# Pooled attention and routed attention experts on one core: queries four tokens to a partition, turned on VectorE, scores in four row tiles

## The chip, the core and the metric

The kernel runs on one core of a Trainium2 chip, in one launch. The metric is the device time in microseconds; a figure for a kernel is the median of its runs. TensorE is called PE, VectorE DVE, ScalarE ACT, GpSimd POOL and SyncE SP, as in the profile.

## What is computed

Two blocks in a row, for B = 8 batches, H = 8 heads, S = 576 tokens and D = 64. The first is attention over keys and values pooled by eight, so 72 keys. Its output, 512 wide, is the input x of the second: four causal attention experts with a head width of 64, of which each token takes the two with the highest gate.

```python
def _attn_ref(q, k, v):
    k_p = k.reshape(B, H, 72, 8, D).mean(axis=3)
    v_p = v.reshape(B, H, 72, 8, D).mean(axis=3)
    attn = softmax(q @ k_p.transpose(0, 1, 3, 2) / 8)
    return attn @ v_p

def _moe_ref(x, w_gate, wq, wk, wv, wo):      # x: (8, 576, 512)
    logits = x @ w_gate                       # 4 experts
    topk = the two highest; w = softmax of their logits
    for e in range(4):
        a = softmax(causal((x @ wq[e]) @ (x @ wk[e]).T / 8))
        out += w[e] (0 where e is not chosen) * (a @ (x @ wv[e]) @ wo[e])
```

## The kernel before

The order of the work is written out by hand: a string SEQ (L561 on) of some 1100 tokens, `name:batch@bank`. Each token calls a small function that issues instructions, and each engine runs its own instructions in the order of the string. A `d` at the end puts a copy on DVE rather than ACT, a `c` cuts a matmul into four column tiles of 32. The whole PSUM is one tile of eight banks, and the number after `@` is the bank that a token's matmuls write. The batches are staggered: while the experts of one batch run, the attention of the next ones is under way.

Per batch, in the order of the data:

- `L` (L109): loads from HBM with a cast to bf16, issued on POOL. Keys and values come in 3 chunks each, two tokens to a partition (96 partitions, 768 pieces of 128 elements a chunk); queries in 6 chunks of 96 tokens, 768 pieces of 64 elements each. Three buffers of each kind (NRAW).
- `PK`/`kc` (L222): pooling as a matmul with a fixed matrix, three column tiles side by side; the 72 pooled keys lie in 96 rows. Then the copy to SBUF. `KT`/`kt` (L237): four flips (matmuls with the identity) turn the pooled keys, two heads at a time, into kpT with 128 rows of head dimensions. `PV`/`vc` do the same pooling for values.
- `Q`/`r` (L246): for each of the four head pairs, six flips of 96 tokens into a PSUM bank, and a copy of 576 columns into qT (24 of the 32 copies on DVE, 8 on ACT).
- `E`/`es` (L255): scores, transposed (keys on partitions). Per head pair two matmuls with 64 rows each, side by side in two row tiles, into two banks; one exp of 1024 elements reads both banks into eta. The 64 tail tokens (512 to 575) of all heads go last: eight matmuls of 64 columns, two exps.
- `D`, `dn`, `dx`, `O`, `ov` (L283 to L319): denominators by a matmul with a constant, their inverse by ln and exp on ACT, the product with the values, and the scaled result into xT.
- `P`/`p` (L390): projections to q and k of the experts; `V`/`vg` (L321): values and gate logits.
- `gate` (`g0` to `g9`, L336): exp of the logits on ACT (`g0`), then on DVE the second highest of four by max and min, a mask, weights and their normalisation: nine more steps.
- `S`/`sb` (L412): the experts' scores, 64-row tiles, exps on ACT; `am` (`a`, L440): causal masks by affine_select on POOL.
- `B` (L466), `bv` (L477): weights times values; on DVE the reciprocal (`bz`), its product with the gate (`bg`, L484) and the scaled copy (`b`, L489).
- `T`/`t`: flips and copies; `Y`/`y`: the output projection, a copy to `ofin`, and the store, on SP's queue.

`H` tokens are warm-up matmuls on zeros that write a bank nobody reads (51 of them, all in the first 25 us). `W` loads the experts' weights on POOL, `c` reorders them. A PE "form" below means the shape in which the array is used: 128 rows by 128 or 32 columns, or 64 rows by 128 columns in two row tiles (E and S). Which form a token has follows from its function: H, KT, Q, T, Y, and P, V without `c`: 128 by 128; PK, PV, D, O, and tokens with `c`: 32-column tiles; E and S: 64-row tiles.

The softmax here doesn't subtract the row's maximum and nothing guards it: scores larger than these inputs give would overflow.

## Time and profile before

| what | value |
|---|---|
| runs, us | 166.84, 167.1, 168.86; median 167.1 |
| span of the profiled execution | 165.0 us |
| last output matmul starts, last store is issued | 160.4 us, 161.2 us |
| granted PE clock, mean | 0.996 |
| busy: PE, ACT, DVE, POOL | 157.0, 135.0, 123.8, 104.9 us |
| DVE: copies of query flips | 24 of 0.45 us |
| ACT: copies of query flips | 8 of 0.65 us |
| ACT: main exps of the pooled scores | 32 of 1.02 us; tails 16 of 0.38 us |
| POOL: load issues | 48 of q at 0.775 us, 48 of k and v at 0.78 us |
| POOL: causal masks | 72 of 0.41 us |
| DMA queue of the loads | 78928 packets, 15.21 MB |

The page gives busy times by engine, forty slices of the span, and groups of instructions by line. A group line has the count, the busy time, the mean of one in ns, and the idle time ahead of it with what ended it. Matmuls overlap: each lasts some 0.2 to 0.4 us from start to end, while the next starts much earlier, so prices on PE are read from start to start in the timeline. The table by stretches gives, for each stretch, its length, then the busy us of PE, PEld (weight loads), DVE, ACT and POOL with the number of instructions, then the granted PE clock, the DMA share and GB/s. About one matmul record in twenty is missing from this trace; counts are therefore taken from the code.

### The profile page before, as it was taken

How to read it: one execution, taken by the hardware profiler on the slowest of the kernel's cores; microseconds unless marked ns; L12 is line 12 of the kernel's file. 1: busy time of each engine (PE TensorE's matmuls, PEld its weight loads, DVE VectorE, ACT ScalarE, POOL GpSimd, SP SyncE). 2: the span in 40 equal slices, each digit the busy share in tenths (PEclk: the TensorE clock that was granted, in tenths of full speed). 3: DMA queues.
4: the chain of work that ended last, by engine and by line, in shares of the span. 5: the costliest groups of instructions: out<-in, count | busy, mean ns of one | idle time of the engine just before them, and what ended most of it. 6: DMA issues, size and time to landing. Idle time of an engine off the chain costs nothing. (4 is left out here: it accounts for less than half of the span.)

```text
span 165.0 us, 6106 instructions
## 1 busy us (share of the span) xinstructions
PE 157.0 (95%) x2463; PEld 93.8 (57%) x2463; DVE 123.8 (75%) x410; ACT 135.0 (82%) x247; POOL 104.9 (64%) x178
## 2 busy tenths in 40 slices
PE   6999988999999999999999999999999999999980
PEld 2344354568557656654754878555647686555730
DVE  1101497589799859976988899998998989779960
ACT  3029758999998999888998997789997999898860
POOL 6999891899999999965959997400140211364100
PEclk9999999999999999999999999999999999999998
DMA  2999999999999999999999999923113043055875
GB/s 22 160 153 171 164 172 178 170 145 139 177 156 173 164 157 148 156 233 217 206 178 226 168 198 83 174 100 86 47 68 127 4 131 127 0 190 195 257 260 191
DMA packets 84204, 25.04 MB, mean 152 GB/s; under 512 B 79312, under 2 KB 79568, under 8 KB 84176
## 3 DMA queue, kind: packets, MB, share of 16 engines
q0 software_dynamic: 78928, 15.21, 110.6%
q1 hardware_dynamic: 5024, 9.05, 15.9%
q8 instruction: 19, 0.31, 0.7%
q10 hardware_dynamic: 224, 0.39, 0.6%
q14 instruction: 9, 0.07, 0.1%
HBM read 30.42 MB, written 9.44 MB: 242 GB/s over the span
## 5 line engine op out<-in xcount | busy, mean ns | idle before, releaser
L433 ACT ACTIVATE etb_97<-psum 128x1024 bf16<-128x1024 f32 x24 | 23.6, 1023 | 2.5 <-PE psum L185 2.4
L433 ACT ACTIVATE etb_98<-psum 128x1024 bf16<-128x1024 f32 x24 | 23.5, 1027 | 1.3 <-PE psum L185 1.1
L450 POOL TENSOR_SCALAR_AFFINE_SELECT etb_98<-etb_98 128x256 bf16<-128x256 bf16 x32 | 12.5, 410 | 17.4 <-ACT etb_98 L433 17.2
L450 POOL TENSOR_SCALAR_AFFINE_SELECT etb_97<-etb_97 128x256 bf16<-128x256 bf16 x32 | 12.4, 415 | 15.8 <-ACT etb_97 L433 15.7
L173 PE MATMUL psum<-warm 128*128 128x512 bf16 x51 | 15.2, 443 | 1.8 <-DVE onesd L146 1.3
L273 ACT ACTIVATE eta_91<-psum 96x1024 bf16<-96x1024 f32 x16 | 15.9, 1018 | 1.1 <-PE psum L185 1.1
L273 ACT ACTIVATE eta_92<-psum 96x1024 bf16<-96x1024 f32 x16 | 15.6, 1020 | 0.7 <-PE psum L185 0.6
L117 POOL DMA_DIRECT2D qraw_68<-in_q_dram x18 | 13.9, 775 | 1.2 <-PE psum L185 1.1
L176 DVE COPY ofin<-psum 128x512 f32<-128x512 f32 (+1 forms) x18 | 11.9, 673 | 3.2 <-PE psum L185 2.4
L117 POOL DMA_DIRECT2D qraw_69<-in_q_dram x18 | 13.8, 770 | 0.5 <-issue 0.5
L176 DVE CAST qk_99<-psum 128x512 bf16<-128x512 f32 (+1 forms) x16 | 10.5, 670 | 3.8 <-PE psum L185 3.6
L176 DVE CAST qk_100<-psum 128x512 bf16<-128x512 f32 (+1 forms) x16 | 10.5, 654 | 3.5 <-PE psum L185 3.5
L176 ACT COPY ofin<-psum 128x512 f32<-128x512 f32 (+1 forms) x19 | 10.7, 580 | 2.7 <-PE psum L185 1.8
L185 PE MATMUL psum<-wvg,xT_96 128*32 128x260 bf16 (+1 forms) x120 | 10.8, 275 | 0.0
L173 PEld LDWEIGHTS <-warm 128*128 128x128 bf16 x51 | 5.1, 111 | 9.5 <-issue 5.8
L185 PE MATMUL psum<-wvg,xT_95 128*32 128x260 bf16 (+1 forms) x156 | 10.5, 275 | 0.0
L185 PEld LDWEIGHTS <-etb_97 128*128 128x128 bf16 x240 | 8.8, 97 | 2.0 <-issue 0.4
L117 POOL DMA_DIRECT2D qraw_70<-in_q_dram x12 | 9.2, 784 | 0.0
L185 PEld LDWEIGHTS <-etb_98 128*128 128x128 bf16 x240 | 8.3, 97 | 1.4 <-issue 0.8
L185 PE MATMUL psum<-qk_100 64*128 64x64 bf16 (+4 forms) x96 | 8.8, 276 | 0.1
L117 POOL DMA_DIRECT2D kraw_71<-in_k_dram x9 | 7.0, 787 | 2.7 <-DMA qraw_70<-in_q_dram 1.8
L185 PE MATMUL psum<-qk_99 64*128 64x64 bf16 (+4 forms) x96 | 8.4, 277 | 0.0
(198 smaller groups left out, 452.8 us busy)
## 6 DMA issues: line engine op xcount, KB each, us to landing
out_dram<-ofin SPq DMA_DIRECT2D x31, 256.0 KB, 3.0
kraw_71<-in_k_dram POOLq DMA_DIRECT2D x9, 192.0 KB, 6.2
qraw_68<-in_q_dram POOLq DMA_DIRECT2D x18, 96.0 KB, 5.3
vraw_74<-in_v_dram POOLq DMA_DIRECT2D x9, 192.0 KB, 5.5
kraw_72<-in_k_dram POOLq DMA_DIRECT2D x9, 192.0 KB, 5.9
qraw_69<-in_q_dram POOLq DMA_DIRECT2D x18, 96.0 KB, 5.5
vraw_75<-in_v_dram POOLq DMA_DIRECT2D x9, 192.0 KB, 4.9
kraw_73<-in_k_dram POOLq DMA_DIRECT2D x6, 192.0 KB, 6.5
```

The lines of the kernel that those rows point to most:

```text
L117: nc.gpsimd.dma_start(out=dst, in_=src)
L173: nc.tensor.matmul(out=psum[:, bank, :], lhsT=warm[:, 0:128], rhs=warm[:], start=True, stop=True)
L176: (nc.vector.tensor_copy if dve else nc.scalar.copy)(out=out, in_=in_)
L185: nc.tensor.matmul(out=out, lhsT=lhsT, rhs=rhs, start=start, stop=stop)
L273: nc.scalar.activation(out=eta[:, hp, :, 0:MAIN], in_=psum[0:KR, bank : bank + 2, :], func=EXP, scale=ATT_EXP_SCALE,)
L433: nc.scalar.activation(out=et[:, ep, :, eo : eo + n], in_=psum[:, bank : bank + 2, 0:n], func=EXP, scale=MOE_EXP_SCALE,)
L450: nc.gpsimd.affine_select(out=blk, in_=blk, pattern=[[0, 2], [1, 128]], compare_op=ISGE, fill=0.0, base=0, channel_multiplier=-1,)
```

## The change

1. Queries are loaded four tokens to a partition (128 partitions, pieces of 256 elements), four heads a load: two loads a batch instead of six. The 64 tail tokens of four batches share one buffer, 32 partitions a batch, one load each.
2. `Q` and `r` are gone. A DVE transpose of 32x32 blocks of 4-byte words (`U`, three for a batch's halves and the shared tails: 18 in all) turns the queries: a word is a pair of neighbouring head dimensions, so each 32-partition group then holds 32 pairs, and the even and odd dimensions lie interleaved in the free dimension.
3. Scores run in four row tiles of 32 rows. Each row tile has the tokens of its own partition group; even and odd dimensions are two accumulating matmuls of 128 columns. A half batch (four heads) is 32 matmuls into four banks, a batch's tails are 16 matmuls of 64 columns in one row tile. Each row tile needs the keys of every head and parity in its own 32 rows, so kpT holds four copies, rotated by 32 rows.
4. For batches 0, 1 and 2 the rotated copies are made by flips (16 instead of 4) from a key buffer that holds the first columns twice (`kd`); for batches 3 to 7 by six small SBUF-to-SBUF DMAs on SP (`R`). PK's columns are sorted into even and odd dimensions.
5. The exps read PSUM in the token order (`j r h p t`), so their reads step 32 elements; main exps keep 1024 elements, tails become one exp of 512.
6. The gate's steps after the exp (except `g7`, `g8`) and `bg` move from DVE to POOL; the mask comes from the differences of all pairs of logits.
7. The staging buffers of the weights lie in the output buffers oT.
8. SEQ is written anew: other places, banks and engines for nearly all tokens. Warm-ups 51 to 40; load tokens 96 to 72. Copies on ACT and DVE, before and after: y 18 and 17, then 21 and 14 (the last one is split on both); p 8 and 32, then 12 and 28; t 3 and 21, then 8 and 16; v 14 and 22, then 10 and 26; kc 5 and 3, then 7 and 1; kt 5 and 3, then 3 and 8; and three kd on DVE.

```diff
-    qraws = bufs(NRAW, [KR, NQC, H, D], BF16, "qraw")
+    qraws = bufs(NRAW, [128, H, QT, D], BF16, "qraw")
+    qtls = bufs(B // QUAD, [128, H, 2, D], BF16, "qtl")
+    qTts = bufs(B // QUAD, [128, H, 2, 32, 2], BF16, "qTt")
     kraws = bufs(NRAW, [KR, 3, H, 2, D], BF16, "kraw")
     vraws = bufs(NRAW, [KR, 3, H, 2, D], BF16, "vraw")
-    kps = bufs(2, [KR, H * D], BF16, "kp")
-    kpTs = bufs(2, [128, NHP, KR], BF16, "kpT")
+    kps = bufs(2, [KR, NHP, 224], BF16, "kp")
+    kpTs = bufs(2, [128, NRG, NHP, KR], BF16, "kpT")
     vps = bufs(2, [KR, H, D], BF16, "vp")
-    qTs = bufs(8, [128, S], BF16, "qT")
-    etas = bufs(2, [KR, NHP, 2, S], BF16, "eta")
+    qTs = bufs(2, [128, H, QT, 32, 2], BF16, "qT")
+    etas = bufs(2, [KR, H, S], BF16, "eta")
...
         if nm == "q":
-            dst = qraws[b % NRAW][:, c, :, :]
-            src = q[b, :, KR * c : KR * (c + 1), :].rearrange("h p d -> p h d")
+            hs = slice(NHP * c, NHP * c + NHP)
+            dst = qraws[b % NRAW][:, hs].rearrange("p h t d -> p h (t d)")
+            src = q[b, hs, 0:MAIN, :].rearrange("h (p t) d -> p h (t d)", t=QT)
+        elif nm == "t":
+            dst = qtls[b // QUAD][32 * c : 32 * c + 32].rearrange("p h t d -> p h (t d)")
+            src = q[b + c, :, MAIN:S, :].rearrange("h (p t) d -> p h (t d)", t=2)
...
-    def pool_pe(b, bank, raw, mat):
+    def pool_pe(b, bank, raw, mat, split):
         for t in range(2):
             for c in range(3):
-                mm(psum[32 * c : 32 * c + 32, bank, :], mat[:, :], raw[:, c, :, t, :],
-                   start=(t == 0), stop=(t == 1))
+                x = raw[:, c, :, t, :]
+                if split:
+                    x = x.rearrange("p h (x u) -> p h u x", u=2)
+                mm(psum[32 * c : 32 * c + 32, bank, :], mat[:, :], x, start=(t == 0), stop=(t == 1))
...
-        copy(dve, kps[b % 2][:], psum[0:KR, bank, :])
+        copy(dve, kps[b % 2][:, :, 0:128], psum[0:KR, bank, :].rearrange("j (a n) -> j a n", a=NHP))
+
+    def kd(b, bank, dve):
+        copy(dve, kps[b % 2][:, :, 128:224], psum[0:KR, bank, :].rearrange("j (a n) -> j a n", a=NHP)[:, :, 0:96])
...
     def KT(b, bank):
-        for hp in range(NHP):
-            flip(half_bank(bank)[:, KR * hp : KR * hp + KR],
-                 kps[b % 2][:, 128 * hp : 128 * hp + 128])
-
-    def kt(b, bank, dve):
-        copy(dve, kpTs[b % 2][:],
-             half_bank(bank)[:, 0 : NHP * KR].rearrange("p (a n) -> p a n", a=NHP))
-
-    def Q(b, bank, hp):
-        for c in range(NQC):
-            flip(half_bank(bank)[:, KR * c : KR * (c + 1)],
-                 qraws[b % NRAW][:, c, 2 * hp : 2 * hp + 2, :].rearrange("p h d -> p (h d)"))
-
-    def r(b, bank, dve, hp):
-        copy(dve, qTs[4 * (b % 2) + hp][:], half_bank(bank)[:, 0:S])
-
-
-    def Es(b, bank, hp):
-        for i in range(NHP) if hp == NHP else [hp]:
-            c0, n, at_ = (MAIN, TAIL, TAIL * i) if hp == NHP else (0, MAIN, 0)
-            for hh in range(2):
-                r0 = hh * D
-                mm(psum[0:KR, bank + hh, at_ : at_ + n], kpTs[b % 2][r0 : r0 + D, i, :],
-                   qTs[4 * (b % 2) + i][r0 : r0 + D, c0 : c0 + n])
-
-    def es(b, bank, dve, hp):
-        eta = etas[b % 2]
-        if hp == NHP:
-            for hh in range(2):
-                nc.scalar.activation(
-                    out=eta[:, :, hh, MAIN:S],
-                    in_=psum[0:KR, bank + hh, 0 : NHP * TAIL].rearrange("p (a n) -> p a n", a=NHP),
-                    func=EXP, scale=ATT_EXP_SCALE,
-                )
-        else:
+        for i in range(NRG if b in TURNED else 1):
+            for hp in range(NHP):
+                c = 32 * (-i % NRG)
+                o = KR * (NHP * (i % 2) + hp)
+                flip(half_bank(bank + i // 2)[:, o : o + KR], kps[b % 2][:, hp, c : c + 128])
+
+    def kt(b, bank, dve, part=0):
+        n = 2 if b in TURNED else 1
+        copy(dve, kpTs[b % 2][:, 2 * part : 2 * part + n],
+             half_bank(bank + part)[:, 0 : n * NHP * KR].rearrange("p (k a n) -> p k a n", k=n, a=NHP))
+
+    def spread(b):
+        for k in range(1, NRG):
+            n = 32 * (NRG - k)
+            for d0, s0, m in ((32 * k, 0, n), (0, n, 128 - n)):
+                nc.sync.dma_start(out=kpTs[b % 2][d0 : d0 + m, k], in_=kpTs[b % 2][s0 : s0 + m, 0])
+
+    def turn(b, i):
+        if i == 2:
+            dst, src = qTts[b // QUAD][:], qtls[b // QUAD][:]
+        else:
+            hs = slice(NHP * i, NHP * i + NHP)
+            dst, src = qTs[b % 2][:, hs], qraws[b % NRAW][:, hs]
+        nc.vector.transpose(out=dst.rearrange("p h s x t -> p (h s x t)").bitcast(U32),
+                            in_=src.rearrange("p h s d -> p (h s d)").bitcast(U32))
+
+    def Es(b, bank, u):
+        def score(r, h, t, out, qT):
+            rows = slice(32 * r, 32 * r + 32)
+            nc.tensor.matmul(
+                out=out, lhsT=kpTs[b % 2][rows, (r - 2 * (h % 2) - t) % NRG, h // 2, :],
+                rhs=qT[rows, h, :, :, t].rearrange("p s x -> p (s x)"),
+                start=(t == 0), stop=(t == 1), tile_position=(32 * r, 0),
+            )
+
+        for h in range(H) if u == NHP else range(NHP * u, NHP * u + NHP):
+            for t in range(2):
+                if u == NHP:
+                    score(b % QUAD, h, t, psum[0:KR, bank, TAIL * h : TAIL * h + TAIL], qTts[b // QUAD])
+                else:
+                    o = 128 * (h % NHP)
+                    for r in range(NRG):
+                        score(r, h, t, psum[0:KR, bank + r, o : o + 128], qTs[b % 2])
+
+    def es(b, bank, dve, u, half=None):
+        if u == NHP:
             nc.scalar.activation(
-                out=eta[:, hp, :, 0:MAIN], in_=psum[0:KR, bank : bank + 2, :],
+                out=etas[b % 2][:, :, MAIN:S].rearrange("j h (p t) -> j h p t", t=2),
+                in_=psum[0:KR, bank, :].rearrange("j (h t p) -> j h p t", h=H, t=2),
+                func=EXP, scale=ATT_EXP_SCALE,
+            )
+            return
+        for r in range(2 * half, 2 * half + 2) if SPLIT else [2 * half]:
+            n = 1 if SPLIT else 2
+            nc.scalar.activation(
+                out=etas[b % 2][:, NHP * u : NHP * u + NHP, 128 * r : 128 * (r + n)].rearrange(
+                    "j h (r p t) -> j r h p t", r=n, t=QT),
+                in_=psum[0:KR, bank + r : bank + r + n, :].rearrange("j r (h t p) -> j r h p t", h=NHP, t=QT),
                 func=EXP, scale=ATT_EXP_SCALE,
             )
 
...
         elif step == 1:
-            L2 = L.rearrange("p c (a b) -> p c a b", b=2)
-            for nm, op in (("hi", MAXOP), ("lo", MINOP)):
-                nc.vector.tensor_tensor(
-                    out=tmp(nm, 2, 1), in0=L2[:, :, :, 0:1], in1=L2[:, :, :, 1:2], op=op
-                )
+            nc.gpsimd.tensor_sub(
+                out=tmp("Df", E, E), in0=L.unsqueeze(3).to_broadcast([128, n, E, E]),
+                in1=L.unsqueeze(2).to_broadcast([128, n, E, E]),
+            )
         elif step == 2:
-            for nm, src, op in (("s2", "hi", MINOP), ("s3", "lo", MAXOP)):
-                nc.vector.tensor_tensor(
-                    out=tmp(nm, 1), in0=got(src)[:, :, 0, :], in1=got(src)[:, :, 1, :], op=op
-                )
+            nc.gpsimd.tensor_scalar(out=got("Df"), in0=got("Df"), scalar1=0.0, scalar2=None, op0=ISLT)
         elif step == 3:
-            nc.vector.tensor_tensor(
-                out=tmp("m2", 1), in0=got("s2"), in1=got("s3"), op=MAXOP
+            nc.gpsimd.tensor_add(
+                out=got("Df")[:, :, :, 0:2], in0=got("Df")[:, :, :, 0:2], in1=got("Df")[:, :, :, 2:4]
             )
         elif step == 4:
-            nc.vector.tensor_tensor(
-                out=tmp("msk", E), in0=L, in1=got("m2").to_broadcast([128, n, E]), op=ISGE
+            nc.gpsimd.tensor_add(
+                out=got("Df")[:, :, :, 0], in0=got("Df")[:, :, :, 0], in1=got("Df")[:, :, :, 1]
             )
         elif step == 5:
-            nc.vector.tensor_mul(out=tmp("W", E), in0=got("Ex"), in1=got("msk"))
+            nc.gpsimd.tensor_scalar(
+                out=tmp("msk", E), in0=got("Df")[:, :, :, 0], scalar1=2.0, scalar2=None, op0=ISLT
+            )
+            nc.gpsimd.tensor_mul(out=tmp("W", E), in0=got("Ex"), in1=got("msk"))
...
         if step == "bz":
             nc.vector.reciprocal(out=rz, in_=o[:, :, :, HD : HD + 1])
         elif step == "bg":
-            nc.vector.tensor_mul(
+            nc.gpsimd.tensor_mul(
                 out=gt[:, :, :, 0], in0=rz[:, :, :, 0],
                 in1=at[b // 2, "G"][:, p0:p1, 2 * ep : 2 * ep + 2].rearrange("p c e -> p e c"),
...
+        I:0 J:0 L_k1:0 K:0 L_k0:0 L_k2:0 H14:0@7 PK:0@7 kc:0 kd:0d H4:0@6 KT:0@6 L_q1:0 M:0 L_q0:0
+        kt1:0d L_t1:0 L_v2:0 U0:0 L_t3:0 kt0:0 H7:0@5 E0:0@4 U1:0 E1:0@0 L_v0:0 e01:0 L_v1:0 e00:0
+        e10:0 L_t0:0 L_t2:0 PV:0@4 vc:0d D0:0@5 e11:0 H3:0@7 O01:0@4 O11:0@0 L_k2:1 d0:0 U2:0 L_k1:1
+        D1:0@1 x0:0 o01:0 d1:0 O00:0@5 x1:0 L_k0:1 E4:0@2 O10:0@3 o10:0 H2:0@7 PK:1@4 kd:1d L_q1:1
+        e4:0 D2:0@7 W1:0 U1:1 O20:0@2 o00:0 kc:1 H3:0@6 KT:1@3 kt0:1 kt1:1d L_q0:1 d2:0 x2:0 W0:0
...
```

## The prediction

> **What bounds the kernel now.** I read the page's busy shares and slices first, then the table by stretches, then PE's timeline, because everything hangs on what PE does between its matmuls. The chain that ended last is of no use here: it covers only the last 1.2 us.

> ```profile
> span 165.0 us, 6106 instructions
> ...
> PE 157.0 (95%) x2463; PEld 93.8 (57%) x2463; DVE 123.8 (75%) x410; ACT 135.0 (82%) x247; POOL 104.9 (64%) x178
> ...
> PE   6999988999999999999999999999999999999980
> ```
> PE is busy from about 30 us to the end. But matmuls overlap, so "busy" hides waits. The table by stretches (busy us of PE, PEld, DVE, ACT, POOL) shows who is near its own limit:

> ```profile
> 24.00:32.00 8.00, 7.34 (x126) 3.90 (x123) 5.75 (x16) 6.85 (x13) 4.24 (x8) 1.00 1.81 176
> ...
> 50.00:60.00 10.00, 9.95 (x139) 6.46 (x140) 8.24 (x29) 8.97 (x17) 9.89 (x17) 1.00 2.00 164
> ...
> 100.00:110.00 10.00, 9.92 (x153) 6.46 (x153) 9.50 (x29) 7.72 (x15) 4.60 (x9) 1.00 1.01 108
> ```
> From 50 to 60 us POOL (loads and masks) is as full as PE; ACT runs at 0.9. PE's timeline gives the real prices, start to start:

> ```profile
> 28.22 0.38 PE L185 MATMUL psum<-xT_95,wkp_122 128*128 128x512 bf16 x1
> 28.53 0.23 PE L185 MATMUL psum<-qk_99 64*128 64x64 bf16 x4
> 28.60 0.21 PE L185 MATMUL psum<-qT_87,kpT_80 64*96 64x64 bf16 x2
> 28.65 0.21 PE L185 MATMUL psum<-qT_88,kpT_80 64*96 64x64 bf16 x2
> 28.69 0.21 PE L185 MATMUL psum<-qT_89,kpT_80 64*96 64x64 bf16 x2
> 28.74 0.21 PE L185 MATMUL psum<-qT_90,kpT_80 64*96 64x64 bf16 x2
> 28.78 0.40 PE L185 MATMUL psum<-qT_89,kpT_80 64*96 64x512 bf16 x2
> 29.11 0.40 PE L185 MATMUL psum<-xT_95,wkp_123 128*32 128x512 bf16 x4
> ```
> and later, from all engines' timeline:

> ```profile
> 73.42 0.44 PE L194 MATMUL psum<-ident,osc_108 128*128 128x128 bf16 x5
> ...
> 73.70 0.61 PE L185 MATMUL psum<-wvg,xT_96 128*128 128x260 bf16 x4
> ```
> A 512-column matmul, or a set of tiles side by side, takes 0.2155 us; a pair of 64-column score tails with 96-column weights 45 ns; a 128-column flip 55 ns (five in 0.28 us). From 28.22 to 28.53 is 0.31 us for one 0.2155 us matmul: going from 128-row to 64-row form costs 94 ns, and the way back at 29.11 about the same. The records hold 97 such changes of form.

> **PE's sum now.** Walking the order string with these prices (96-column flip 42 ns, 65-column matmul 29 ns, 260 columns 111 ns): P 31.2 us, V 16.0, Y 15.5, B 14.1, warm-ups 51 x 0.2155 = 11.0, S 10.8, E 8.3, Q 192 x 0.042 = 8.1, O 7.5, PK and PV 6.9, T 4.4, D 3.8, KT 1.3: 139.0 us, and 97 changes x 0.1 = 9.7: 148.7 us. Set against the recorded starts, PE's lateness (start minus work so far) is 1.3 us at the start, 6.8 at the first projection (26.23 us), 7.2 at 40 us and 11.8 at the last output matmul (160.03 us). So PE bounds, behind a ramp fed by the loads.

> [...] here only two row tiles are seen, starting 3 ns apart. [...] no row of this trace reads PSUM with a stride at length.

> **The change on PE.** Query flips go: -8.1 us. Main scores: per batch 4 pairs x 0.2155 = 0.86 us become 16 sets of four 128-column tiles x 55 ns = 0.88: +0.1 over all. I take 55 because the 45 ns of weights seen in the tails fit under it; if weights and matmul add (45 + 53), it is +5.5 us. Tails: 4 pairs x 45 ns become 16 matmuls in one row tile, one after another, x 45 ns: 0.72 - 0.18 = 0.54 a batch, +4.3. Turned keys: 12 more flips in three batches, 36 x 42 ns = +1.5. Warm-ups 51 to 40: -2.4. The new order has 115 changes of form instead of 97 (scores no longer share a form with the experts' scores): +1.8. Sum -2.7: 146.0 us. PK's sorted columns I leave at 0.2155. A half batch of scores now holds four of the eight banks, two of them for two exps (2.0 us), where a pair held two for one; the flips' bank goes instead. I put nothing for it, since the order gives PE other matmuls meanwhile; without them each of the 16 would cost up to 1 us.

> **The loads.** These set the ramp.

> ```profile
> 1.36 2.42 POOL L117 DMA_DIRECT2D kraw_71<-in_k_dram  x3 [0.85 <-POOLq L689]
> ...
> 4.05 4.59 POOL L117 DMA_DIRECT2D qraw_68<-in_q_dram  x6
> 8.64 2.29 POOL L117 DMA_DIRECT2D vraw_74<-in_v_dram  x3
> ```
> The packets between 2 and 40 us come at 0.175 MB/us where they are 256 bytes (k, v, weights) and 0.154 where 128 (q); a batch of k, q or v is 0.59 MB. That puts k at 8.0, q at 11.9 (PE's last wait for it ends at 12.20), v at 15.2 (PV at 15.9), the q weights at 23.9 (copied at 24.46): the stream, not its issue, is the limit. New q packets are 512 bytes; not seen, between 0.175 and 0.21; I take 0.187. Then q lands at 10.8, but the tails of four batches (0.26 MB) come before v ends (14.9), k of batch 1 at 19.1, its second half of q at 20.5, the k weights at 22.0. Behind that lie PK 0.4, copy 0.6, flips 0.7, copy 0.8: first projection at about 23.3 us, 2.9 earlier. But later loads bind too (the same rates, going on down the list of L and W tokens), because the new order puts all keys of batch 3 before half of batch 2's queries: keys of 2 at 33.1 against 25.4 us of PE work ahead of them, keys of 3 at 37.9 against 30.0, queries of 2 at 39.3 plus a turn against 32.0, values of 2 at 45.1 against 37.1. Lateness is then 8.3 at about 40 us, not 7.2: +1.1.

> **The other engines.** DVE: 24 query copies x 0.45 = -10.8; gate steps -12.7 and bg -6.4 (36 x 0.18) go to POOL; 18 turns are added. [...] the 128x512 f32 copy takes 0.687 us: 18 x 0.69 = +12.4 (at twice that, +24.8: still below now). With moved copies (y, p, t, v: -4.4; kc, kd, kt, c: +3.5) about 105 of 123.8. ACT: 8 query copies x 0.65 = -5.2, tail exps 16 x 0.38 to 8 x 0.59 = -1.4, moved copies +4.3: about 133 of 135. POOL: 48 query loads x 0.775 become 24 of about 0.73 (a 256-descriptor load took 0.712): -19.7; each batch gains eight gate instructions and 36 bg in all. [...] Even. These cost nothing while B's results wait behind the 0.9-full ACT and other PE work[...]. What queues behind a waiting bg on POOL is masks and loads; behind the masks waits B. DVE's 15% relief should take as much off the late drift: 0 net. SP: 5 x 6 small copies of keys; first scores follow the key copy by 6.6 us of PE work or more, against 3.0 us of landing for outputs: hidden; beyond 6.6 us each adds to E. Weight staging in oT is free: oT is first written by flips of batch 0's output, long after the weights are copied out.

> **Sum.** -2.7 + 1.1 = -1.6 us: the profiled execution goes from 165.0 to 163.4. The median of the runs is 2.1 us above its span, so 167.1 becomes 165.5.

> **Rivals.**
> - *Likeliest, 165.5 (own range 163 to 168), chance 0.50*: as summed.
> - *The ramp and the waits shrink, 162.5, 0.26*: 512-byte packets at 0.21 take 0.3 us off each half batch and lateness stays at 7.2; the drift of 4.6 us to the end falls to 3 with DVE at 105 and fewer loads ahead of masks: -2.7 - 0.2 - 1.6 = -4.5. For: POOL 9.89 of 10 at 50 us. Against: ACT is as full as before.
> - *Strided exps, slower, 0.14*: the 32 main exps read PSUM four bytes in every 128. ACT's rows (0.59 us for 512, 1.02 for 1024 elements) give 0.84 ns an element; a halved rate adds 0.86 x 32 + 3 = 30 us, ACT 163 us from 12 us on: about 180. ACT has some 16 us of idle time, scattered; from about 1.3 us an exp it decides. Against: no engine row here shows such a loss.
> - *Row tiles do not run together, 0.08*: 64 x 55 ns a batch instead of 16 is +21 us: 186; break-even is 21 ns more per set of four.
> - Rest 0.02.

> **Numbers.** About 2% (3.3 us) is what a measurement of this kernel tells from no change. Below 163.8: 0.16 of the first case and nearly all of the second: 0.33. Above 170.4: the last cases, 0.21. Between: 0.46. The range 160 to 172 leaves out the two slow mechanisms at full size and little of the second case.

> **What would show it.** Right: sets of four score tiles 55 ns apart; tails 45; 115 changes at 94 ns; first projection near 23.3 us; lateness near 8.3 at 40 us and 12 to 13 at the end; exps at 1.02 us; turns at 0.69. Wrong: exps above 1.1, sets above 75 ns, POOL gaps ended by PSUM work with loads late behind them, or E waiting for SP's copies.

## The result, and the profile after

The changed kernel takes 177.7 us (median of four runs, 176.93 to 179.18) against 167.0 before: 1.062 times, 95% interval 1.056 to 1.068. It is slower. The prediction was 165.5, with a range from 160 to 172. Medians and ranges are over all runs of a kernel; ratios leave out runs over 1.5% above its fastest.

The page of the changed kernel, busy shares and slices (PE, then the granted clock):

```profile
span 175.2 us, 7382 instructions
...
PE 157.3 (90%) x3108; PEld 96.5 (55%) x3108; DVE 110.9 (63%) x299; ACT 136.4 (78%) x234; POOL 108.3 (62%) x254
...
PE   7686999987499799999699979999999999999980
...
PEclk9969999999999999999999999999999999999998
```
DVE, ACT and POOL have 3 to 6 us more than was worked out for them (about 105, 133 and 105 us), and none is full. PE is no longer busy throughout from 30 us on: slices 10, 11, 14, 20 and 24 have holes. The same stretches as before:

```profile
24.00:32.00 8.00, 8.00 (x220) 4.98 (x220) 5.38 (x14) 6.18 (x10) 5.13 (x7) 1.00 1.85 180
50.00:60.00 10.00, 9.03 (x165) 5.13 (x163) 6.29 (x13) 9.70 (x17) 7.97 (x20) 1.00 1.48 168
100.00:110.00 10.00, 8.97 (x258) 5.72 (x247) 7.18 (x18) 8.09 (x18) 2.89 (x8) 1.00 0.81 101
```
A microsecond of PE is gone from each of the two later stretches. Only ACT is fuller there than before (9.70 of 10 us from 50 to 60), and it isn't what PE waits for: the chain of waits gives ACT 1%. This chain, which before covered 1.2 us, now reaches back through nearly the whole span, and names what releases PE:

```profile
PE 72%; DMA 14%; POOL 4%; issue 3%; DVE 2%; ACT 1%; SPq 1%; DVEq 0%; POOLq 0%
```
PE's timeline has the places. A bracket gives the idle time ahead of the instruction and what ended it; lines that don't matter are left out:

```profile
17.46 0.40 PE L199 MATMUL psum<-vraw,poolv 96*32 96x512 bf16 x3 [1.58 <-ACT eta L311]
...
34.58 0.30 PE L199 MATMUL psum<-eta,vp 96*32 96x64 bf16 x15
35.59 0.62 PE L199 MATMUL psum<-eta,vp 96*32 96x64 bf16 x9 [0.71 <-issue]
...
40.36 0.50 PE L199 MATMUL psum<-wvg,xT 128*32 128x260 bf16 x9
41.78 0.40 PE L199 MATMUL psum<-wvg,xT 128*32 128x260 bf16 x7 [0.92 <-issue]
...
45.29 0.66 PE L286 MATMUL psum<-qT,kpT 32*96 32x128 bf16 x31
48.26 0.21 PE L286 MATMUL psum<-qT,kpT 32*96 32x128 bf16 x1 [2.31 <-issue]
...
58.48 0.32 PE L286 MATMUL psum<-qT,kpT 32*96 32x128 bf16 x8 [0.52 <-DMA kpT<-kpT]
...
85.02 0.27 PE L286 MATMUL psum<-qTt,kpT 32*96 32x64 bf16 x2 [1.64 <-DMA kpT<-kpT]
...
101.91 0.41 PE L199 MATMUL psum<-kraw,poolk 96*32 96x512 bf16 x3 [0.99 <-DMA kraw<-in_k_dram]
```
Four kinds of hole: in the ramp PE waits for the exps of the first scores; later it stops in the middle of a token, after 15, 9 and 31 matmuls of one kind, and waits for nothing that the profile names ("issue"); it waits for SP's copies of keys; it waits for the load of keys of batch 7.

The clock row has a 6 in slice 3, where the row of the kernel before has nines up to its last slice. From 8 to 16 us (the clock is the third figure from the end), before:

```profile
8.00:16.00 8.00, 7.83 (x71) 3.88 (x72) 0.46 (x1) 4.61 (x7) 8.00 (x11) 1.00 1.97 161
```
And after, with the warm-ups and the flips that fall into it:

```profile
8.00:16.00 8.00, 6.42 (x95) 3.53 (x95) 3.54 (x12) 1.90 (x3) 5.73 (x9) 0.79 1.67 179
...
10.28 1.89 PE L187 MATMUL psum<-warm 128*128 128x512 bf16 x4
11.96 1.37 PE L208 MATMUL psum<-ident,kp 96*128 96x96 bf16 x16
```
In the trace PE runs at half the clock for 3.4 us, from 9.6 to 13.1 us. It has just waited 2.10 us for the first keys, up to 9.46 us. The four warm-ups take 1.68 us up to the start of the flips. In e12 (below), where the keys come at 9.50 us and the clock stays whole, the same four take 0.87 us:

```profile
10.03 1.04 PE L187 MATMUL psum<-warm 128*128 128x512 bf16 x4
10.90 1.14 PE L208 MATMUL psum<-ident,kp 96*128 96x96 bf16 x16
```

The DMA issues, median us from issue to landing, show loads later than before, and copies of keys beyond the 3.0 us that I had for them. Before, keys took 5.9 to 6.5 us and values 4.9 to 6.9, by buffer:

```profile
kraw_71<-in_k_dram POOLq DMA_DIRECT2D x9, 192.0 KB, 6.2
...
vraw_74<-in_v_dram POOLq DMA_DIRECT2D x9, 192.0 KB, 5.5
```
And after:

```profile
kraw<-in_k_dram POOLq DMA_DIRECT2D x24, 192.0 KB, 6.9
vraw<-in_v_dram POOLq DMA_DIRECT2D x24, 192.0 KB, 7.1
...
kpT<-kpT SPq DMA_DIRECT2D x10, 72.0 KB, 5.0
```

Lateness of PE (start minus work so far at the prediction's prices), worked out as in the prediction, in us:

| at | before | after | e5 uncut | e6 mended | e8: before, no late loads | e12: e6, no late loads |
|---|---|---|---|---|---|---|
| 26 us | 6.8 | 10.6 | 11.4 | 9.3 | 6.4 | 10.0 |
| 40 | 7.1 | 11.9 | 11.7 | 10.0 | 7.7 | 10.4 |
| 50 | 7.2 | 15.9 | 12.3 | 10.1 | 8.0 | 10.8 |
| 60 | 7.5 | 17.4 | 14.1 | 11.8 | 8.0 | 11.6 |
| 80 | 8.2 | 18.3 | 16.4 | 17.4 | 8.6 | 12.4 |
| 110 | 9.4 | 22.5 | 19.0 | 18.7 | 9.8 | 13.2 |
| first of the last output matmuls | 11.8 | 24.2 | 20.7 | 20.4 | 12.2 | 14.9 |

### The profile page after: what moved, and what is told of

Read it like the earlier page. It is cut to its first block, busy times and chain, and to the rows that moved or that the text cites. A ratio compares the mean times of both kernels' runs of the same rounds, so it can differ in the third digit from the quotient of the medians.

```text
span 175.2 us, 7382 instructions
## 1 busy us (share of the span) xinstructions
PE 157.3 (90%) x3108; PEld 96.5 (55%) x3108; DVE 110.9 (63%) x299; ACT 136.4 (78%) x234; POOL 108.3 (62%) x254
## 4 chain that ended last, share of the span: by engine, by line
PE 72%; DMA 14%; POOL 4%; issue 3%; DVE 2%; ACT 1%; SPq 1%; DVEq 0%; POOLq 0%
PE psum L199 56%; PE psum L286 8%; DMA kraw<-in_k_dram 7%; DMA kpT<-kpT 7%; PE psum L208 4%; PE psum L187 4%; POOL kraw L130 1%; ACT eta L311 1%; POOL vraw L130 1%; POOL etb L488 1%; SPq L272 1%; DVE xT L356 0%; DVE qT L280 0%; DVE kp L190 0%; DVE ofin L190 0%
## 5 line engine op out<-in xcount | busy, mean ns | idle before, releaser
L471 ACT ACTIVATE etb<-psum 128x1024 bf16<-128x1024 f32 x48 | 47.9, 1036 | 2.7 <-PE psum L199 1.8
L311 ACT ACTIVATE eta<-psum 96x1024 bf16<-96x1024 f32 x32 | 31.0, 1016 | 9.0 <-PE psum L286 9.0
L488 POOL TENSOR_SCALAR_AFFINE_SELECT etb<-etb 128x256 bf16<-128x256 bf16 x64 | 24.9, 405 | 3.5 <-ACT etb L471 3.3
L190 DVE CAST qk<-psum 128x512 bf16<-128x512 f32 (+1 forms) x28 | 17.5, 630 | 12.7 <-PE psum L199 11.5
L199 PE MATMUL psum<-wvg,xT 128*32 128x260 bf16 (+1 forms) x420 | 22.6, 275 | 0.9 <-issue 0.9
L356 DVE TENSOR_TENSOR xT<-psum,rza 128x512 bf16<-128x512 f32 x32 | 21.0, 681 | 3.1 <-ACT rza L338 1.4
L130 POOL DMA_DIRECT2D vraw<-in_v_dram x24 | 19.0, 793 | 3.9 <-PE psum L199 1.9
L199 PE MATMUL psum<-wop,oT 128*128 128x512 bf16 (+2 forms) x104 | 20.6, 376 | 0.0
L199 PE MATMUL psum<-xT,wkp 128*32 128x64 bf16 (+3 forms) x272 | 19.9, 272 | 0.0
L199 PE MATMUL psum<-vaug,etb 128*128 128x65 bf16 x480 | 19.9, 193 | 0.0
L199 PE MATMUL psum<-xT,wqp 128*32 128x512 bf16 (+3 forms) x332 | 19.8, 290 | 0.0
L199 PE MATMUL psum<-qk 64*128 64x64 bf16 (+4 forms) x192 | 17.4, 278 | 0.0
L199 PE MATMUL psum<-eta,vp 96*32 96x512 bf16 (+1 forms) x256 | 14.6, 289 | 0.7 <-issue 0.7
L286 PE MATMUL psum<-qT,kpT 32*96 32x128 bf16 x512 | 11.4, 218 | 3.3 <-issue 2.3
```

The costliest lines, as they stand in the source:

```text
L130: nc.gpsimd.dma_start(out=dst, in_=src)
L190: (nc.vector.tensor_copy if dve else nc.scalar.copy)(out=out, in_=in_)
L199: nc.tensor.matmul(out=out, lhsT=lhsT, rhs=rhs, start=start, stop=stop)
L286: nc.tensor.matmul(out=out, lhsT=kpTs[b % 2][rows, (r - 2 * (h % 2) - t) % NRG, h // 2, :], rhs=qT[rows, h, :, :, t].rearrange("p s x -> p ...
L311: nc.scalar.activation(out=etas[b % 2][:, NHP * u : NHP * u + NHP, 128 * r : 128 * (r + n)].rearrange("j h (r p t) -> j r h p t", r=n, t=Q ...
L356: nc.vector.tensor_tensor(out=xT[:, 2 * g + t, mcols(b)], in0=psum[:, bank, :], in1=rz[:, g, 0:MAIN], op=MULT)
```

## The experiments

My theory after the result: (a) PE's own instructions come late while the loads run; (b) SP's copies of keys aren't hidden; (c) loads land late, first in the ramp, then for batch 7. The rivals are named in each expectation. Figures are medians; the kernel before took 167.5, 167.6, 167.6 and 168.0 us beside the four groups (e1 to e4, e5 to e8, e9 to e11, e12 to e14).

**e1, no copies of keys on SP.**
```
-  lhsT=kpTs[b % 2][rows, (r - 2 * (h % 2) - t) % NRG, h // 2, :]
+  lhsT=kpTs[b % 2][rows, (r - 2 * (h % 2) - t) % NRG if b in TURNED else 0, h // 2, :]
-  R:3 R:4 R:5 R:6 R:7
```

> The changed kernel without the copies of keys on SP: for batches 3 to 7 every row tile reads the first, unrotated copy of the keys, so the scores of these batches are wrong, but the number, the shape and the order of all matmuls stay. The other two theories (PE's own instructions arrive late; loads arrive late) leave the rest as it is. If SP's copies cost what the trace shows, the waits at E1:3 (57.6 us, 0.9 us) and E0:5 (83.2 us, 1.7 us) go and the kernel falls from 177.7 to about 175.1. If these waits only cover others that stand behind them, the time stays within 1 us. The stops at 34.7, 40.6 and 45.7 us must stay as they are.

175.35 us: 2.3 less than the changed kernel, as expected. The copies are a cost of their own. PE still stops without a name, after the same 15 and 31 matmuls (38.19 and 50.58 us).

**e2, keys of batch 7 earlier.**
```
-  L_v2:7 ... L_q0:7 ... L_k1:7 ... L_k0:7 ... L_k2:7
+  L_k0:7 ... L_q0:7 L_k2:7 ... L_k1:7 ... L_v2:7
```

> The changed kernel with the three loads of the keys of batch 7 issued some 8 us earlier on POOL, in exchange for loads of values of batch 7. If POOL's line of gate steps ahead of these loads is what made PE stop at 100.5 to 101.9 us (2.1 us in all), that stop goes and the kernel falls to about 175.7. If PE would there have met another late thing (queries of batch 7, values of 6), the time stays at 177.7.

177.13 us (175.02 to 179.17): too wide to tell from no change. In the profiled execution the wait at 100 us is gone (lateness 20.4 at 100 us, 20.8 at 110, where the changed kernel goes from 20.6 to 22.5). The local mechanism holds; a gain in time isn't shown.

**e3, six more warm-ups, twelve more PE instructions.**
```
-  H14:0@7 PK:0@7
+  H20:0@7 PK:0@7
```

> The changed kernel with 20 instead of 14 warm-up matmuls ahead of the first keys: six more, 12 more PE instructions, in time in which PE waits for keys anyway (7.0 to 9.4 us). If PE stops at 34.7, 40.6 and 45.7 us because the next 16 KB of its own instructions have not come, the three stops stay 256 instructions apart and sit 12 instructions (six matmuls) earlier in the order: the last one after 25 score matmuls of E0:2, not after 31, and the one before after 3 value matmuls, not 9. If the stops belong to what the instruction at that place needs (a bank, a buffer), they stay at the same instruction. The time changes by under 1 us; the granted clock in the ramp may rise and take up to 1 us off.

177.83 us, the same as the changed kernel. PE's timeline of e3 at two of the stops:

```profile
34.23 0.26 PE L199 MATMUL psum<-eta,vp 96*32 96x64 bf16 x9
36.43 0.67 PE L199 MATMUL psum<-eta,vp 96*32 96x64 bf16 x8 [1.94 <-issue]
...
46.57 0.59 PE L286 MATMUL psum<-qT,kpT 32*96 32x128 bf16 x25
49.09 0.32 PE L286 MATMUL psum<-qT,kpT 32*96 32x128 bf16 x7 [1.93 <-issue]
```
15 has become 9, and 31 has become 25: six matmuls earlier, to the matmul. (The middle stop didn't occur in this execution. Its clock stays whole in the ramp but falls to half for 3.4 us from 36.2 and from 49.9 us, about where these two stops end.) So a stop doesn't belong to an instruction or its data, but to a count. Counted from the order string, each matmul with its weight load as two, the stops of the changed kernel come after 958, 1214 and 1470 instructions: 256 apart. The DMA queues of the two pages say what 256 is. Before (packets, MB, share of 16 engines):

```profile
q8 instruction: 19, 0.31, 0.7%
```
And after:

```profile
q8 instruction: 24, 0.39, 1.0%
```
These are packets of 16 KB. The traces record 4932 instructions of PE before and 6222 after, so 0.31 and 0.39 MB are 63 bytes for each, and a packet of 256 instructions would have 64 for each. From these figures and the distance of the stops I take it that queue 8 carries PE's instructions, 256 to a packet. The stops of the changed kernel last 0.71, 0.92 and 2.31 us. In the packets' times, a packet of queue 8 starts at 33.13, 39.33 and 45.81 us, and PE goes on 2.45 or 2.46 us after each.

**e4, no loads of keys, values and queries of batches 3 to 7.** (all `L_k`, `L_v`, `L_q` tokens of these batches taken out)

> The changed kernel without the loads of keys, values and queries of batches 3 to 7: their buffers keep what batches 0 to 2 left there, so the output is wrong from batch 3 on, while all other work stays. The loads end at about 35 us. If late instructions are a matter of a loaded DMA system, the stops at 40.6 and 45.7 us (3.2 us) go; SP's copies of keys land sooner than 5 us and their waits (2.6 us) go for the most part; the wait for keys of batch 7 (2.1 us) goes. Together about 170. If the stops come from the density of PE instructions alone, they stay and the time is about 173. If none of the three costs what I put it at, 176 or more.

170.44 us, as expected of the three causes together. The stop at 34.7 us, while loads still run, stays; the two later ones and the wait for batch 7 are gone; SP's copies land in 2.0 to 2.3 us:

```profile
kpT<-kpT SPq DMA_DIRECT2D x10, 72.0 KB, 2.0
```

**e5, fewer PE instructions in the load phase.**
```
-  P_q1:0@7c P_q0:0@0c P_t0:0@2c V0:0@1c V2:0@3c P_t0:1@2c V1:0@7c V3:1@6c V2:1@4c P_q1:1@6c
+  the same ten without c
```

> The changed kernel with ten tokens between 26 and 47 us (projections and values of batches 0 and 1) as 128-wide matmuls and not cut into four column tiles: the same sums, 384 PE instructions (1.5 fetches of 256) less in that stretch, eight changes of form more (+0.8 us). If late instructions are what stops PE there, the stops of 3.9 us shrink to under 1 us and the kernel falls by about 3, to 174.7. If the stops belong to the loads or buffers of that stretch, they stay and the time rises to 178.5.

175.16 us: 2.5 less. All three stops are gone (lateness 12.3 at 50 us, not 15.9); one comes at 74.9 us.

**e6, mended.**
```
+  R right behind kt (all batches); KT:3 kt:3d R:3 ahead of E0:2
+  U0:0 ahead of kt1:0d, pads behind U1:0; e2's loads; e5's ten tokens
```

> The changed kernel with e5's ten tokens uncut, SP's copies of keys placed right behind the copy they read (for batch 3 also its flips ahead of the scores of batch 2), the keys of batch 7 loaded earlier, and the first turned queries ahead of the memsets of pads on DVE. If the costs that the trace shows add up (fetches 3.1 net, copies 2.3, keys of batch 7 up to 1.5, ramp 0.7), it falls from 177.7 to about 170. If one hides another, 172 to 174. It does not reach the 167.5 of the kernel before, since 3 us of the ramp stay.

174.51 us, not 170. Up to 50 us the mends work (lateness 10.1). Then PE, now earlier, meets later loads, and a stop after 2238 instructions:

```profile
73.38 0.31 PE L199 MATMUL psum<-qk 64*128 64x320 bf16 x2
75.31 0.26 PE L199 MATMUL psum<-qk 64*128 64x192 bf16 x2 [1.61 <-issue]
...
76.85 1.91 PE L199 MATMUL psum<-xT,wkp 128*128 128x512 bf16 x4
78.70 0.71 PE L199 MATMUL psum<-qk 64*128 64x512 bf16 x6
```
The clock is at half from 76.2 to 79.6 us, behind the stop: the four projections at 76.85 us take 1.85 us, where four at the price of 0.2155 take 0.86. Lateness grows by 1.8 us in the stop and by 1.2 behind it.

**e7, the kernel before with more PE instructions.**
```
-  P_t0:0@6 P_t0:1@7 V3:1@6 V0:1@0 V2:1@7 V1:1@2 P_q0:0@0 P_k0:0@1
+  the same eight with c
```

> The kernel before with eight tokens between 26 and 50 us cut into four column tiles: the same sums and the same time of matmuls (64 cut tail matmuls take 0.5 us, as 16 uncut ones do), 336 PE instructions more in that stretch, three changes of form more (+0.3 us). If late instructions are a matter of how many PE instructions are due while the loads run, this kernel gets stops without a name too, 256 instructions apart, and loses 1.5 to 4 us. If the stops come from something that only the changed kernel has (its score matmuls, its loads of 512-byte packets), it stays within 0.5 us of 167.5.

169.48 us, ratio 1.013 (1.007 to 1.019). The kernel before, which had no such stop, gets one:

```profile
30.73 0.39 PE L185 MATMUL psum<-xT,wqp 128*32 128x512 bf16 x2
32.76 1.04 PE L185 MATMUL psum<-xT,wqp 128*32 128x512 bf16 x14 [1.65 <-issue]
```
It comes after 702 instructions. 702, 958, 1214, 1470 and 2238 all leave 190 when divided by 256. Neither the score matmuls nor the new loads are needed for a stop: 336 more PE instructions in the load phase were enough.

**e8, the kernel before without the same late loads: the control of e4.**

> The kernel before without the loads of keys, values and queries of batches 3 to 7 (wrong output from batch 3 on, all other work stays): the control of e4, which gained 7.2 us of 177.7 by the same. If the kernel before hides its loads, it gains 1 us or less: 166.5 to 167.5. If loads weigh on any kernel of this kind, by POOL's time or the DMA system, it gains as much as e4 and the difference of the two kernels is not a matter of loads.

166.9 us, ratio 0.996 (0.995 to 0.998). The kernel before hides its late loads but for 0.7 us; the changed one pays 7.2 us for them.

**e9, gate and bg on DVE.** (the gate's steps and `bg` as in the kernel before, all else as changed)

> The changed kernel with the gate's steps and bg as before, on DVE (part 6 of the change undone). POOL loses some 25 us of work, DVE gains about 19 (to 130). If POOL's line of small steps holds up the loads behind it, loads are issued earlier, the wait for keys of batch 7 (2.1 us) goes and the kernel falls by 1 to 3 us, to 175 to 176.5. If the exchange is even, as the prediction had it, it stays within 0.7 us of 177.7; if DVE is the scarcer of the two it rises to 179.

179.43 us (177.88 to 181.95); by the ratio, 1.061 (1.052 to 1.070), even with the changed kernel. POOL falls from 108.3 to 86.1 us, DVE rises to 122.6, and PE then waits 1.7 us for xT from DVE, up to 124.4 us. Moving POOL's small steps back to DVE brings no gain.

**e10, queries in quarters.**
```
+  for h0 in (NHP * c, NHP * c + 2):
+      hs = slice(h0, h0 + 2)
       ...
       nc.gpsimd.dma_start(out=dst, in_=src)
```

> The changed kernel with each load of half a batch's queries (0.26 MB) issued as two of two heads: the same packets, 16 more load issues on POOL (+11 us of its time). If loads land late because more bytes are under way at once (a load of POOL waits for an earlier one to land, and each load now brings more), the median landing of keys and values falls from 7 us to about 6, PE's stops shrink below 3 us and the time falls by 0 to 2 us in spite of POOL's extra work. If the stream's rate alone sets the landings, they stay at 7 us, and POOL's extra work makes it 178 to 180.

175.2 us, 2.5 less, although POOL works 11 us more (119.0). Keys and values land earlier:

```profile
kraw<-in_k_dram POOLq DMA_DIRECT2D x24, 192.0 KB, 6.0
vraw<-in_v_dram POOLq DMA_DIRECT2D x24, 192.0 KB, 5.7
```
The stops did not shrink as expected (1.58 and 1.64 us, 3.2 together). In the profiled execution the gain comes between 80 and 110 us, where lateness grows by 1.4 (19.5 to 20.9) and in the changed kernel by 4.2. The earlier landings are shown; that they bring this gain is argued.

**e11, e6 with the gate on DVE.**

> The mended kernel of e6 (174.5 us) with the gate's steps and bg on DVE. If POOL's small steps are what makes the loads late that e6 meets between 60 and 80 us (7 us of lateness), it falls to 170 to 172. If they are late because the stream is full, it stays within 1 us of 174.5.

175.11 us, the same as e6. The profiled execution is the longest of five (177.74 us), and the two profiles can't be set against each other as they are: lateness at 80 us is 14.2 against e6's 17.4, but 3.0 of this is e6's stop with the half clock behind it; at 130 us it is 22.3 against 19.3, after a wait of PE for DVE and 3.4 us at half clock (from 123.2 us) that e6 doesn't have there. Whether POOL's steps delay loads in e6 isn't shown.

**e12, e6 without late loads: the closing of the account.**

> The mended kernel of e6 without the loads of keys, values and queries of batches 3 to 7 (wrong output from batch 3 on): the closing of the account. With no late loads there are no stops, no late copies of keys and no late loads; what is left against e8 (166.9, the kernel before without the same loads) is PE's own sum (146.5 against 148.2) and the ramp (lateness 9.3 against 6.8 at 26 us). So it should come to 167 to 168, equal to e8 within 1 us. If the changed order itself (banks, engines) costs more than ramp, stops, copies and loads, it stays above 169.

169.6 us, ratio 1.007 (1.003 to 1.010): by the ratios 1.8 us above e8, where I expected 1 at most, so by its words the expectation missed. In the profiled executions the last output matmuls start at 161.36 against 160.41 us, and the table has where it comes from: lateness differs by 3.6 at 26 us; after that it grows by 4.9 here and by 5.8 in e8. It is the ramp, larger here than in e6 (10.0, not 9.3), and not the order behind it. The other part is the clock. Of the twenty executions the seven with a mean clock of 0.991 to 0.996 take 168.0 to 169.0 us (the profiled one is of these, and has no stretch at half clock before its end), the others, at 0.970 to 0.989, 169.2 to 172.4; one stretch of 3.4 us at half clock lowers the mean by 0.010. All executions of e8 are at 0.993 or more.

**e13, e6 with queries in quarters.**

> The mended kernel of e6 (174.5) with the queries' loads in quarters as in e10: the best of the changed kernels that the runs so far point to. If fewer bytes under way bring what they brought in e10 (2.5 us), 172; if e6 already has that gain by its other mends, 174. It does not reach 167.5.

175.5 us (174.57 to 177.58): nothing beyond e6. The mends don't add up. No version of the changed kernel came below the kernel before.

**e14, the first keys alone on the stream.**
```
   KT:0@6
+  N:0
   L_q1:0
...
+  elif name == "N":
+      nc.gpsimd.tensor_copy(out=seen[:], in_=kraws[0][:, :, 0, 0, 0:4])
```

> The changed kernel with POOL reading the first keys (twelve elements a partition, 0.1 to 0.2 us) before it issues any load of queries, so that the first keys have the stream to themselves. If the first keys land at 9.4 us and not at 8.0 because loads under way share the stream, they now land by 8.2 (as in the kernel before, where queries are issued more slowly); queries then land some 2 us later than 12.4, and the time is 177 to 179. If the keys are limited by themselves, they still land at 9.4.

180.06 us. The time is above the 177 to 179 that I expected; in the profiled execution the clock is at half from 14.6 to 28.3 us. PE's pooling of the last of the first keys starts at 9.46 us in the changed kernel, from 8.84 to 10.30 us in the other nine profiled executions with the same first loads (e1 to e6, e9, e11, e12), and at 8.07 us here (POOL's read follows at 8.20 us and takes 0.19). The scores then wait for queries:

```profile
8.07 0.60 PE L200 MATMUL psum<-kraw,poolk 96*32 96x512 bf16 x4 [0.98 <-DMA kraw<-in_k_dram]
...
15.08 1.22 PE L287 MATMUL psum<-qT,kpT 32*96 32x128 bf16 x37 [2.96 <-DVE qT L281]
```
So the first keys are late because queries under way share the stream with them.

## Why the prediction was wrong, point by point

The prediction's sum was -2.7 us of work on PE and +1.1 us of lateness. The first term came true; the second was 12.4 us. What failed is the path by which loads reach PE in the ramp and behind it, and three terms that the prediction put at nothing or left out: PE's instructions, SP's copies of keys, and the banks that the scores hold.

**The change on PE (-2.7): right.** Score sets, tails, turns and exps came in as priced. Most sets of four score matmuls follow each other at 55 to 60 ns in the trace (55 predicted), so the row tiles run together; 16 tails take 0.72 us, 45 ns each. From the page's groups, turns and main exps (mean ns after the busy time):

```profile
L311 ACT ACTIVATE eta<-psum 96x1024 bf16<-96x1024 f32 x32 | 31.0, 1016 | 9.0 <-PE psum L286 9.0
...
L280 DVE STREAM_TRANSPOSE qT<-qraw 128x512 uint32<-128x512 uint32 x16 | 10.9, 694 | 0.0
```
Both slow rivals, strided exps and row tiles one after another, are out. e12 shows the sum as a whole: without the late loads, lateness after the ramp grows no more than in the kernel before.

**A term was left out: PE's instructions themselves (3.9 us).** I counted PE's time and not its instructions. By the order string matmuls and weight loads rise from 4926 to 6216, mostly in bursts (64 in 0.5 us for a half batch of scores), while the loads fill the DMA engines (nine tenths or more in slices 2 to 14 of the page's DMA row). (Both traces hold each of these, so the remark above that one matmul record in twenty is missing doesn't hold.) Shown by e3, e5 and e7; e5, which takes out 384 of them, gains 2.5 us.

**"Hidden" for SP's copies: wrong (2.6 us).** I set 6.6 us of PE work against the 3.0 us of a store's landing. But six issues follow one another on SP, the last of batch 3 at 53.2 us where the copy of its keys was done by 49.2, and a copy lands 4.1 to 5.0 us after its issue (medians by size), 5.3 and 6.4 us where PE waited for it; without the late loads 2.0 to 2.3 (e4). Shown by e1 and e4.

**The ramp (first projection 23.3): wrong; it came at 26.90.** Lateness there is 10.6. The stream's rate was about right: where nearly all packets are of 512 bytes they come at some 0.18 MB/us (the 0.187 of the prediction was an assumption). The step that failed is to take each load as landing in its turn. A query load now brings 0.26 MB for one issue of 0.77 us, so more is under way at once, and all of it shares the stream: keys 9.4 us and not 8.0, queries 12.4 and not 10.8 (POOL waits 0.75 and 0.80 us for landings of queries, the second time up to 12.42), weights of k about 24.8 and not 22.0. e14 shows the first of these. Behind it come two waits of the order that I didn't see: the second copy of keys on DVE waits for the first on ACT (10.99 us), and the first turn waits behind pads and that chain (13.84 us). e6 moved the turn, and its lateness at 26 us is 1.3 less, but the turn isn't the reason: e11 has the same order, keys at 9.45 us and the clock at half from 10.5 to 13.9 us, and its lateness is 10.6 as in the changed kernel; e12 has the same order, keys at 9.50 us and the clock whole, and has 10.0. So 0.6 of the 1.3 us goes with the clock, and 0.7 with e6's first keys, at 9.02 us.

**Nothing for the scores' banks: wrong in the ramp (1.6 us).** I put nothing for the four banks of a half batch, since the order gives PE other matmuls meanwhile. In the ramp it has none: by the order string the first two half batches fill all eight banks, the pooled values come next, and PE waits 1.58 us for the exps of the first (17.46 us). The kernel before has no such wait at its first pooled values; e6 and e12 have it with 1.41 us each. It is part of the ramp's lateness and stands nowhere else in the span. No run takes it out, so what it costs in the end isn't shown.

**"Lateness 8.3 at 40 us", later loads +1.1: too small.** It was 11.9, then 15.9 at 50 us with the stops. By 50 us 8.26 MB of loads had landed against 7.45 before, but by 70 us 10.5 in both: POOL's issues, between masks, steps and buffers still in use, may then set the pace; no run settles it. The wait for keys of batch 7 (2.1 us at 101 us, 0.6 regained) is of this kind.

**POOL "even", drift 0 net: right as far as it goes.** "Even" was my estimate. In the trace the 64 gate steps take 16.6 us and the 36 of bg 7.3, and POOL is busy for 108.3 us, 104.9 before. e9 undoes it at no gain.

**The account.** The last output matmuls start at 169.75 and not 160.03 us: 12.4 us of lateness less 2.7 of work. The 12.4 are ramp 3.8, stops 3.9, copies 2.6, keys of batch 7 1.5, and 0.6 of small ones. They aren't independent: the mends for stops, copies and batch 7's wait together (e6) gave 3.2 us. Of the 7.3 us by which e6's lateness grows between 50 and 80 us, 3.0 are a new stop with the half clock behind it. What holds the rest, POOL's pace or loads that share the stream, isn't settled: e10 speaks for the stream, e11 for neither.

## What to carry to other kernels

Count an engine's instructions as well as its time. Here PE, by my reading, ran out of instructions three times, for 0.71, 0.92 and 2.31 us, where many small matmuls fell into the stretch in which loads fill the DMA engines, and the profile shows it only as "issue" in the middle of a run of equal matmuls, 256 instructions apart. Look at how much a load puts under way per issue: with queries at 0.26 MB an issue, keys and values landed after 6.9 and 7.1 us, with half of that after 6.0 and 5.7 (e10), although the stream as a whole was faster than before (8.26 MB by 50 us against 7.45). Price a small copy by its landing in the stretch where it will run, with its issues in a row, not by a row from a quiet stretch: the copies of keys landed after 4.1 to 5.0 us here, after 2.0 to 2.3 without the late loads (e4). A wait that other matmuls are to cover needs a look at the ramp, where there may be none. And compare the granted clock of two executions before their waits: a stretch at half clock can pass for the effect of an edit, as in 0.6 of e6's 1.3 us at 26 us.
